# Attention row maxima: the third one of a step as two 256-key halves, one on each half of TensorE

## The chip, the cores and the metric

The kernel runs on one core of a Trainium2 chip. The metric is the device time of one execution in microseconds (us), the median over several runs. Engines are called as in the profile: PE is TensorE (PEld its weight loads), DVE VectorE, ACT ScalarE, POOL GpSimd, SP the engine that issues most DMAs.

## The reference

Two layers of two sublayers each run over one activation of 2048 tokens by 512 features: a Fourier mixing sublayer (phase A below) and a multi-query attention (phase B). All arithmetic is float32. The attention has 32 query heads of width 16 that share one key head and one value head:

```python
q = (x @ wq).reshape(B, S, H, Dh).transpose(0, 2, 1, 3)
k = x @ wk
v = x @ wv
scores = jnp.einsum("bhqd,bkd->bhqk", q, k) * (Dh ** -0.5)
p = softmax(scores)
o = jnp.einsum("bhqk,bkd->bhqd", p, v)
x = x + o.transpose(0, 2, 1, 3).reshape(B, S, H * Dh) @ wo      # x was layer-normalised before
```

The softmax needs the largest score of every query row and head before the exponentials: 2048 x 32 row maxima over 2048 keys each.

## The kernel before

**Tiling.** The 2048 queries are 16 tiles of 128 rows. The 32 heads are 16 pairs (`NPAIR`): the query tile of a pair holds one head of it (g = 0) on partitions 0 to 63 and the other (g = 1) on partitions 64 to 127. The key tile `kz` is there twice in the same way. So a score matmul contracts over 64 partitions and uses one half of PE's rows, and a matmul of the other head can run beside it on the other half.

**Two passes over the scores.** A first set of matmuls, with queries as weights and keys streaming, serves the maxima alone: `max_half` (lines 347 to 351) computes 128 queries x 512 keys of one head into a PSUM bank (L350), and DVE reduces the bank to one column of the partial maxima `mxp` (L351). Some maxima are computed in phase A (`max_pair`, L336 and L338). When a query tile has all its partials, `max_neg` reduces and negates them, and `max_rows` turns them with a PE transpose (L379) and writes them by DMA into spare rows of the query tile, so that the second pass has them subtracted by the matmul itself. The second pass, with keys as weights and queries streaming, computes transposed scores (`score`, L773), ACT takes the exponential of two of them in one instruction of 128 x 1024 (L776) into a probability tile, and `pv` (L787) multiplies it with the values: four matmuls of 32 columns in each of two parts, eight in the profile, which use all 128 rows of PE.

**Steps.** Phase B is a loop of 512 steps a layer, 32 steps for each query tile (`phase_b`, line 908). A step handles one block of 128 keys and 16 of the heads. PE's program order in it is: the `pv` of the step two before; then the step's group of scores and maxima; then whatever tasks are due. The group is written out in lines 924 to 929:

```python
g = units[o.done][2] if o.done < len(units) else 1
for j, m in ((1 - g, 1), (g, 2), (3 - g, 0), (2 + g, 1)):
    score(i, s_, j)
    for _ in range(m):
        if owed(n) >= 1:
            more_max()
```

Scores 0 and 1 form the first ACT instruction of the step, 2 and 3 the second; `j % 2` is the half of PE. `units` (line 738) lists the maxima still owed, heads alternating, and `owed` allows three of them a step. So a group is: score on half 1-g, maximum on g, score on g, maximum on 1-g, maximum on g, score on 1-g, score on g: four matmuls on half g and three on the other, and the halves change roles from step to step. In the last tile, once the maxima are used up, scores 2 and 3 go to single banks (L766, L768).

**PSUM.** The eight banks are two pairs for the scores (`pair`, tag x; so scores 2 and 3 of a step need the pair that ACT read for scores 2 and 3 of the step before), three single banks (`bank`, tag y) for maxima, transposes and the output projection, and one for `pv` (tag z). A bank is given to the next tile of its tag when the last reader is done; `o_proj` (line 842) holds one y bank while it takes four maxima through the other two.

**Tasks beside the steps.** `half_tasks` and `out_tasks` (lines 959 to 970) list, by step of a tile, the work on finished query tiles: storing and reloading the attention output by SP's DMAs, its scaling and its split into two parts on POOL (`o_scale` L827, `o_hi` L833 and L834), the projection on PE at step 12 (`o_proj`, L86 to L88), the residual (`o_add`, L852) and the output DMA (L853; on POOL's queue in the first layer, on SP's in the second), and in the first layer the next layer norm (`o_stats`, `o_rstd`, `o_ln`, `o_xnh`, `o_xnl`: L166 to L182, L898, L902). `max_neg` comes at step 27 and `max_rows` at step 29, for the first and last query tile in two halves of eight head pairs. DVE, ACT, POOL and SP each work through their own queue in program order.

## Time and profile before

| | |
|---|---|
| three timed runs | 3717.65, 3720.38, 3726.05 us; median 3720.38 us |
| the profiled execution | 3724.12 us, its span 3722.3 us |
| phase B of the two layers (first `pv` to last) | 692.0 to 1864.4 us and 2542.7 to 3711.4 us of the span |
| mean granted PE clock | 0.990 of full speed; 1.00 in phase B |

The profile gives busy time and instruction counts by engine, groups of instructions by line with the mean duration of one, what ended an engine's idle time, and a timeline. In the timeline a row is one run of like instructions: start, length until the last one's end, engine, line, output and inputs, and how many. A matmul's row starts when it may enter PE; its end is modelled. "x" and "y" in the names are the bank tags; `slot` and `xnl` are query or probability tiles.

### The profile page before, as it was taken

Reading aid. Unit: us, or ns where it says so; the run is one execution under the profiler, and the core shown is the slowest. Engines: PE = TensorE matmul, PEld = TensorE weight load, DVE = VectorE, ACT = ScalarE, POOL = GpSimd, SP = SyncE. Lnnn points to the kernel's source line nnn. Section 1 sums busy time; section 2 is a strip of 40 time slices with the busy share of each in tenths; the row PEclk is TensorE's granted clock in tenths of the full one; section 3 lists DMA queues with packets and bytes.
Section 4 is the critical chain, followed back from the end, with each engine's and each line's share of the span. In section 5 each row is a group of like instructions: output and inputs, shape, how many; then the busy total and the mean of one; then the engine's idle time right before and its main releaser. Section 6 shows DMA issues by size and latency. Waiting matters only on the chain. (4 is left out here: it accounts for less than half of the span.)

```text
span 3722.3 us, 64512 instructions
## 1 busy us (share of the span) xinstructions
PE 3631.1 (98%) x25474; PEld 1909.3 (51%) x25474; DVE 2798.4 (75%) x4767; ACT 2400.3 (64%) x3104; POOL 777.3 (21%) x984
## 2 busy tenths in 40 slices
PE   8999999999999999999999999999999999999999
PEld 6786768533433333334377766684343334333333
DVE  5167978788888888888311779778888888888882
ACT  4322222688888888888933231227888888888888
POOL 5534332111111111111154342421000000000000
PEclk9999999999999999999999999999999999999999
DMA  5444241311111100110143342313111111001100
GB/s 176 133 136 125 97 119 52 101 32 50 33 36 31 49 22 24 33 47 23 40 131 104 129 124 92 110 64 89 47 33 36 33 49 34 22 22 50 33 24 25
DMA packets 204736, 243.00 MB, mean 65 GB/s; under 512 B 36880, under 2 KB 160784, under 8 KB 197264
## 3 DMA queue, kind: packets, MB, share of 16 engines
q1 hardware_dynamic: 199504, 222.08, 20.1%
q0 software_dynamic: 4864, 16.78, 1.5%
q8 instruction: 199, 3.26, 0.4%
q14 instruction: 105, 0.86, 0.1%
q10 hardware_dynamic: 64, 0.02, 0.0%
HBM read 174.58 MB, written 63.17 MB: 64 GB/s over the span
## 5 line engine op out<-in xcount | busy, mean ns | idle before, releaser
L776 ACT ACTIVATE slot<-x 128x1024 f32<-128x1024 f32 x1990 | 1943.1, 1027 | 334.4 <-PE x L773 265.5
L351 DVE TENSOR_REDUCE mxp<-y 128x1 f32<-128x512 f32 x3040 | 1908.1, 684 | 281.5 <-PE y L350 233.3
L787 PE MATMUL z<-slot,v 128*32 128x512 f32 x8192 | 1096.3, 605 | 1.9 <-ACT row L790 1.9
L773 PE MATMUL x<-slot,kz 64*128 64x512 f32 x2956 | 900.9, 447 | 3.6 <-DMA slot<-mt 3.5
L773 PEld LDWEIGHTS x<-slot,kz 64*128 64x128 f32 x2956 | 375.3, 185 | 731.5 <-ACT slot L776 598.5
L350 PE MATMUL y<-kz,slot 64*128 64x512 f32 x2208 | 726.2, 435 | 4.8 <-ACT mt L381 0.7
L338 DVE TENSOR_REDUCE mxe<-y 128x1 f32<-128x512 f32 x832 | 516.4, 682 | 189.4 <-PE y L336 184.7
L660 PE MATMUL x<-ch,xnh 64*128 64x512 f32 (+1 forms) x2048 | 507.8, 390 | 16.3 <-DVE slot L74 8.9
L660 PE MATMUL x<-ch,xnl 64*128 64x512 f32 (+1 forms) x2048 | 475.2, 369 | 0.0
L660 PE MATMUL x<-cl,xnh 64*128 64x512 f32 (+1 forms) x2048 | 474.7, 369 | 0.0
L350 PEld LDWEIGHTS y<-kz,slot 64*128 64x128 f32 x2208 | 349.5, 185 | 94.5 <-DVE mxp L351 27.5
L827 POOL TENSOR_TENSOR row<-row,row 128x256 f32<-128x256 f32 x63 | 46.3, 735 | 1677.8 <-DMA row<-rd 1422.6
L336 PE MATMUL y<-kz,slot 64*128 64x512 f32 (+1 forms) x1088 | 354.3, 420 | 33.7 <-DVE mxe L338 20.7
L78 POOL TENSOR_TENSOR cl<-craw,ch 128x512 fp32r<-128x512 f32 x236 | 303.1, 1303 | 289.2 <-ACT ch L77 229.3
L787 PEld LDWEIGHTS z<-slot,v 128*32 128x32 f32 x8192 | 163.6, 108 | 277.3 <-issue 249.2
L660 PEld LDWEIGHTS x<-ch,xnh 64*128 64x128 f32 x2048 | 268.7, 189 | 69.2 <-issue 16.4
L660 PEld LDWEIGHTS x<-ch,xnl 64*128 64x128 f32 x2048 | 280.7, 189 | 33.3
L660 PEld LDWEIGHTS x<-cl,xnh 64*128 64x128 f32 x2048 | 281.7, 190 | 28.0
L77 ACT CAST ch<-craw 128x512 fp32r<-128x512 f32 x256 | 154.8, 620 | 161.8 <-PE x L660 89.5
L666 ACT COPY junk<-x 128x2 f32<-128x2 f32 x256 | 40.5, 158 | 332.3 <-PE x L660 253.6
L336 PEld LDWEIGHTS y<-kz,slot 64*128 64x128 f32 x1088 | 171.8, 188 | 129.4 <-DVE mxe L338 90.5
L338 DVE TENSOR_REDUCE mxp<-y 128x1 f32<-128x512 f32 (+1 forms) x256 | 144.4, 617 | 24.7 <-PE y L336 21.5
(148 smaller groups left out, 3141.7 us busy)
## 6 DMA issues: line engine op xcount, KB each, us to landing
craw<-ct_in SPq DMA_DIRECT2D x112, 512.0 KB
slot<-qd SPq DMA_DIRECT2D x44, 1024.0 KB
qd<-row SPq DMA_DIRECT2D x144, 128.0 KB
od<-row SPq DMA_DIRECT2D x252, 64.0 KB
row<-x_in SPq DMA_DIRECT2D x32, 256.0 KB
mid<-row POOLq DMA_DIRECT2D x32, 256.0 KB, 2.4
craw<-ct_in SPq DMA_DIRECT2D x32, 256.0 KB
row<-mid SPq DMA_DIRECT2D x32, 256.0 KB
```

Of the source, the lines that this page charges most:

```text
L77: nc.scalar.copy(hi, raw)
L78: (eng or nc.vector).tensor_sub(lo, raw, f(hi))
L336: nc.tensor.matmul(pm[g], o.qT[i][gs, pr, :], kz[gs, c0:c0 + n], start=True, stop=True)
L338: nc.vector.reduce_max(to[:, g:g + 1], pm[g], axis=AX.X)
L350: nc.tensor.matmul(pm, o.qT[i][gs, pr, :], kz[gs, kb * 512:kb * 512 + 512], start=True, stop=True)
L351: nc.vector.reduce_max(partial(i)[:, pr, g, kb:kb + 1], pm, axis=AX.X)
L660: nc.tensor.matmul(z[d][:, cols], w, hl[j][t == 1][rs_], start=m == 0 and ph == 0 and j == t == 0, stop=j == 1 and t == 2 and (ph == 0 or ...
L666: nc.scalar.copy(junk, zp[dd][:, :, cols.start])
L773: nc.tensor.matmul(st["e"][:, g, :], kz[64 * g:64 * g + KR, c * P:(c + 1) * P], o.qT[i][64 * g:64 * g + KR, cp:cp + 4, :], start=True, sto ...
L776: nc.scalar.activation(ptiles[i, s_][:, 2 * w:2 * w + 2, :], st.pop("e"), AF.Exp, scale=DH ** -0.5)
L787: nc.tensor.matmul(a[32 * j:32 * j + 32, :], v1[:, c, :], pt[:, j, :], start=c == 0, stop=c == NT - 1)
L827: nc.gpsimd.tensor_mul(bt["ot"][:, cs], bt["ot"][:, cs], bt["den"][:, cs])
```

## The change

The third maximum of a step is replaced. A step now takes one whole pair of maxima, 512 keys for both heads of a pair (`max_both`, or `max_half` for each head), and one couple: 256 keys for both heads, the two results side by side in one y bank, reduced by one DVE instruction to two columns of the partials (`max_couple`). The fourth 512-key block of each tile but the first is done in couples ("split"), the others whole; the partials get a fifth column for the second 256 keys. The two matmuls of a couple write one bank from the two halves of PE, and the second is held back until the first is complete: a `nop` on POOL's queue waits for the first matmul, and the second matmul waits for the `nop` (`behind_`).

The group's order becomes: score 0, score 1, whole maximum on half 0, couple on half 1, score 3, score 2, whole maximum on half 1, couple on half 0. In steps named by `alone`, where POOL has other work queued, there is no couple: the old order is used, with one maximum of an "odd" pair, whose other head follows in a later such step. `pick_pair`, `pick_couple` and `pick_odd` choose the work; `pick_pair` also takes two halves as a whole 512-key block if a tile's due step ("at") comes too near.

Beside that: `o_scale` and `o_hi` come in one step (28 and 10 in place of 27/29 and 9/10), `o_ln` and `o_xnh` in step 25 and `o_xnl` in 26; the output DMA is an `o_out` of its own at step 13 on SP's queue; query tile 14 has its maxima turned in two halves too; a new partial tile has its fifth column set by a POOL memset; two small tiles (`ktmp`, `ms`) use the memory of others. The end of phase A takes its twelve maxima as six pairs. The core of the diff:

```diff
+HALVED = (0, NT - 2, NT - 1)
...
+    def behind_(later, first):
+        tc.add_manual_dep(later.ins, first.ins.name,
+                          mybir.DependencyInfo(mybir.DependencyClass.Sync, mybir.DependencyReason.DATA), reason="row halves")
...
 
         def partial(i):
             if i not in o.mxp:
-                o.mxp[i] = sb.tile([P, NPAIR, 2, 4 if i else 5], F32, name=f"mxp{i % 4}")
+                o.mxp[i] = sb.tile([P, NPAIR, 2, 5], F32, name=f"mxp{i % 4}")
+                if i:
+                    nc.gpsimd.memset(o.mxp[i][:, :, :, 4:5], -3.0e38)
                 for e, (i_, kb, *_) in enumerate(KEPT):
                     if i == i_:
                         nc.gpsimd.tensor_copy(o.mxp[i][:, :, :, kb], st["mxe"][:, e])
...
             gs = slice(64 * g, 64 * g + KR)
             nc.tensor.matmul(pm, o.qT[i][gs, pr, :], kz[gs, kb * 512:kb * 512 + 512], start=True, stop=True)
             nc.vector.reduce_max(partial(i)[:, pr, g, kb:kb + 1], pm, axis=AX.X)
+
+        def max_couple(i, pr, kb, h, g):
+            if g:
+                st["couple"] = bank("y").rearrange("p (g c) -> p g c", g=2)
+            gs = slice(64 * g, 64 * g + KR)
+            c0 = 512 * kb + 256 * h
+            mm = nc.tensor.matmul(st["couple"][:, g, :], o.qT[i][gs, pr, :], kz[gs, c0:c0 + 256], start=True, stop=True)
+            if g:
+                st["relay"] = nc.gpsimd.nop()
+                behind_(st["relay"], mm)
+            else:
+                behind_(mm, st.pop("relay"))
+                nc.vector.reduce_max(partial(i)[:, pr, :, 4 if h else kb], st.pop("couple"), axis=AX.X)
 
         def qT_load(i, k=None):
             k_ = QSLOT[i] if k is None else k
...
-        def max_neg(i, p0=0, n=NPAIR, k=4):
+        def max_neg(i, p0=0, n=NPAIR, k=5):
...
-            ms = sb.tile([P, 2, 2, NPAIR], F32, name="ms").rearrange("p g r a -> p (g r a)")
-            ms = ms[:, :4 * n].rearrange("p (g r a) -> p g r a", g=2, r=2)
+            ms = half(0 if i or p0 else 2)[:, :4 * n].rearrange("p (g r a) -> p g r a", g=2, r=2)
...
         early = {e[:2] for e in EARLY}
-        units = [(0, pr, g, 3) for pr in range(HALF, NPAIR) for g in range(2)]
-        units += [(i, pr, g, kb) for i in range(1, NT) for pr in range(NPAIR) for kb in range(4) for g in range(2)
-                  if (i, kb) not in early]
-        o.done = o.extra = 0
-
-        def more_max():
-            if o.done < len(units) and units[o.done][0] in o.loaded | {0}:
-                max_half(*units[o.done])
-                o.done += 1
-
-        def owed(n):
-            return min(3 * (n + 1) + 12 + o.extra, len(units)) - o.done
+        groups = {}
+        for i in range(NT):
+            for hf in range(2) if i in HALVED else (None,):
+                prs = range(NPAIR) if hf is None else range(HALF * hf, HALF * hf + HALF)
+                if i or hf:
+                    kbs = [kb for kb in range(4) if (i, kb) not in early] if i else [3]
+                    at = NSTEP * i + NT - AHEAD if hf else NSTEP * (i - 1) + NSTEP - AHEAD
+                    groups[i, hf] = {"at": at, "whole": [(pr, kb) for pr in prs for kb in kbs if kb < 3 or not i],
+                                     "split": [(pr, 3, h) for pr in prs for h in range(2) if i]}
+
+        def in_reach(j, n):
+            return j in o.loaded | {0} and (j <= 1 or n >= NSTEP * max(0, j - 4 if j < 13 else j - 2) + 8)
+
+        def alone(n):
+            i, s_ = divmod(n, NSTEP)
+            if i == 0 and 12 <= s_ < 20 or s_ == 29 or i > 0 and s_ == 11:
+                return True
+            return not last and i > 0 and s_ in (17, 18, 26, 27)
+
+        def pick_pair(n, until=0):
+            due = 0
+            for (j, _), g in groups.items():
+                if not in_reach(j, n):
+                    return None
+                if g["at"] < until:
+                    continue
+                if g["whole"]:
+                    pr, kb = g["whole"].pop(0)
+                    return j, pr, kb
+                due += len(g["split"])
+                if due > g["at"] - n and len(g["split"]) > 1:
+                    pr = g["split"].pop()[0]
+                    g["split"].pop()
+                    return j, pr, 3
+            return None
+
+        def pick_couple(n):
+            for (j, _), g in groups.items():
+                if not in_reach(j, n):
+                    return None
+                if g["split"]:
+                    return j, *g["split"].pop(0)
+            return None
+
+        def pick_odd(n):
+            if "odd" in st:
+                return *st.pop("odd"), 1
+            pick = pick_pair(n, next((m for m in range(n + 1, n + NSTEP) if alone(m) or m > 448), n + 1))
+            if pick:
+                st["odd"] = pick
+                return *pick, 0
+            return None
+
+        def max_both(j, pr, kb):
+            for g in range(2):
+                max_half(j, pr, g, kb)
 
         def done_with(i, pr):
-            return all(u[:2] > (i, pr) for u in units[o.done:])
+            if "odd" in st and st["odd"][0] <= i and st["odd"][1] <= pr:
+                return False
+            return not any(q <= pr for (j, _), g in groups.items() if j <= i for q, *_ in g["whole"] + g["split"])
+
+        def all_done():
+            return not any(g["whole"] or g["split"] for g in groups.values()) and "odd" not in st
 
         ptiles = {}
 
...
-            if i == NT - 1 and jj == 1 and o.done == len(units):
+            if i == NT - 1 and jj == 1 and all_done():
...
                 o_mm(k)
                 if k % 2 and i < NT - 1:
-                    for _ in range(2):
-                        more_max()
-                        o.extra += 1
+                    pick = pick_pair(NSTEP * (i + 1) + 12)
+                    if pick:
+                        max_both(*pick)
             o_add(i)
 
         def o_add(i):
             nc.vector.tensor_add(bt["x"], bt["po"], bt["x"])
-            (nc.sync if last else nc.gpsimd).dma_start(dst[i], bt["x"])
+
+        def o_out(i):
+            nc.sync.dma_start(dst[i], bt["x"])
 
         def finish():
             i = NT - 1
...
                 if len(behind) == 2:
                     pv(*behind.pop(0))
                 behind.append((i, s_))
-                g = units[o.done][2] if o.done < len(units) else 1
-                for j, m in ((1 - g, 1), (g, 2), (3 - g, 0), (2 + g, 1)):
-                    score(i, s_, j)
-                    for _ in range(m):
-                        if owed(n) >= 1:
-                            more_max()
+                whole = pick_pair(n)
+                couple = None if alone(n) else pick_couple(n)
+                if not couple:
+                    odd = pick_odd(n)
+                    g = odd[3] if odd else 1
+                    score(i, s_, 1 - g)
+                    if whole:
+                        max_half(*whole[:2], g, whole[2])
+                    score(i, s_, g)
+                    if whole:
+                        max_half(*whole[:2], 1 - g, whole[2])
+                    if odd:
+                        max_half(*odd[:2], g, odd[2])
+                    score(i, s_, 3 - g)
+                    score(i, s_, 2 + g)
+                else:
+                    score(i, s_, 0)
+                    score(i, s_, 1)
+                    if whole:
+                        max_half(*whole[:2], 0, whole[2])
+                    max_couple(*couple, 1)
+                    score(i, s_, 3)
+                    score(i, s_, 2)
+                    if whole:
+                        max_half(*whole[:2], 1, whole[2])
+                    max_couple(*couple, 0)
                 if i == 0 and 2 <= s_ <= 8 and s_ % 2 == 0:
                     q_half_store(14, s_ // 2 - 1)
                 if n == 12:
...
-                for at, j, p0, np_ in ((NT - AHEAD, i, HALF, HALF), (NSTEP - AHEAD, i + 1, 0, HALF if i == NT - 2 else NPAIR)):
-                    if j in (0, NT - 1) or j == i + 1 < NT:
+                for at, j, p0, np_ in ((NT - AHEAD, i, HALF, HALF),
+                                       (NSTEP - AHEAD, i + 1, 0, HALF if i + 1 in HALVED else NPAIR)):
+                    if j in HALVED or j == i + 1 < NT:
...
-                            assert done_with(j, p0 + np_ - 1)
-                            max_neg(j, p0, np_)
+                            assert done_with(j, p0 + np_ - 1), (n, j, p0, groups)
+                            max_neg(j, p0, np_, 5 if j else 4)
...
         def half_tasks(i):
             return {
                 18: [lambda: o_store(i, 0)], 19: [lambda: o_sum(i, 0)], 22: [lambda: o_inv(i, 0)],
-                23: [lambda: o_load(i, 0)], 27: [lambda: o_scale(i, 0)], 29: [lambda: o_hi(i, 0)],
+                23: [lambda: o_load(i, 0)], 28: [lambda: o_scale(i, 0), lambda: o_hi(i, 0)],
             }
 
         def out_tasks(i):
             return {
                 1: [lambda: o_store(i, 1), lambda: o_sum(i, 1), lambda: x_load(i)], 5: [lambda: o_inv(i, 1)],
-                6: [lambda: o_load(i, 1)], 9: [lambda: o_scale(i, 1)], 10: [lambda: o_hi(i, 1)],
-                12: [lambda: o_proj(i)], 14: [lambda: o_stats(i)], 16: [lambda: o_rstd(i)],
-                25: [lambda: o_ln(i)], 26: [lambda: o_xnh(i)], 27: [lambda: o_xnl(i)],
+                6: [lambda: o_load(i, 1)], 10: [lambda: o_scale(i, 1), lambda: o_hi(i, 1)],
+                12: [lambda: o_proj(i)],
+                13: [lambda: o_out(i)], 14: [lambda: o_stats(i)], 16: [lambda: o_rstd(i)],
+                25: [lambda: o_ln(i), lambda: o_xnh(i)], 26: [lambda: o_xnl(i)],
             }
 
         woh = wol = osp = None
```

More of the change, by code (lines that the diff above doesn't have):

```diff
@@ L100, in fnet_mqa_kernel @@
     kmask = sb.tile([P, 1], F32, name="kmask")
-    t_ = sb.tile([P, 1], F32, name="ktmp")
+    t_ = junk[:, :1]
     nc.vector.tensor_reduce(kone[:64], ident[:64, M0:M0 + 2], op=ALU.add, axis=AX.X)
@@ L730, in phase_a @@
                     v_tr(12, 4, vt[0])
-            max_neg(0, 0, HALF, 5)
-            for k in range(12):
-                more_max()
-                if k == 2:
+            max_neg(0, 0, HALF)
+            for k in range(6):
+                max_both(*pick_pair(0))
+                if k == 1:
                     max_rows(0, 0, HALF, nc.scalar)
         early = {e[:2] for e in EARLY}
-        units = [(0, pr, g, 3) for pr in range(HALF, NPAIR) for g in range(2)]
-        units += [(i, pr, g, kb) for i in range(1, NT) for pr in range(NPAIR) for kb in range(4) for g in range(2)
-                  if (i, kb) not in early]
@@ L879, in finish @@
             o_add(i)
+            o_out(i)
         o.finish = finish
```

1 line of the change is left out of this document (removed).

## The prediction

> **What bounds the kernel now.** I read the page first: the shares of the engines and the costliest groups.
>
> ```profile
> PE 3631.1 (98%) x25474; PEld 1909.3 (51%) x25474; DVE 2798.4 (75%) x4767; ACT 2400.3 (64%) x3104; POOL 777.3 (21%) x984
> ...
> L776 ACT ACTIVATE slot<-x 128x1024 f32<-128x1024 f32 x1990 | 1943.1, 1027 | 334.4 <-PE x L773 265.5
> L351 DVE TENSOR_REDUCE mxp<-y 128x1 f32<-128x512 f32 x3040 | 1908.1, 684 | 281.5 <-PE y L350 233.3
> L787 PE MATMUL z<-slot,v 128*32 128x512 f32 x8192 | 1096.3, 605 | 1.9 <-ACT row L790 1.9
> ```
>
> PE looks like the bound, and eight L787 matmuls a step make 8192 / 8 = 1024 steps, and by the table above phase B is 2341 of the 3722 us. But overlapping matmuls make a busy share say little, so I went to the timeline of one step in the second layer (start, length, engine, line, count):
>
> ```profile
> 3003.89 0.39 PE L773 MATMUL x<-slot,kz 64*128 64x512 f32 x1
> ...
> 3003.93 0.18 PEld L350 LDWEIGHTS y<-kz,xnl 64*128 64x128 f32 x1
> 3004.12 1.89 DVE L351 TENSOR_REDUCE mxp<-y 128x1 f32<-128x512 f32 x3 [0.24 <-PE x L773]
> 3004.24 0.19 PEld L773 LDWEIGHTS x<-slot,kz 64*128 64x128 f32 x2
> 3004.24 0.51 PE L773 MATMUL x<-slot,kz 64*128 64x512 f32 x2
> 3004.38 1.94 ACT L776 ACTIVATE slot<-x 128x1024 f32<-128x1024 f32 x2 [0.19 <-PE y L350]
> ...
> 3004.68 1.06 PE L787 MATMUL z<-slot,v 128*32 128x512 f32 x8
> ...
> 3005.68 0.50 PE L773 MATMUL x<-slot,kz 64*128 64x512 f32 x1
> ...
> 3005.68 0.49 PE L350 MATMUL y<-kz,xnl 64*128 64x512 f32 x1
> ...
> 3006.02 0.39 PE L773 MATMUL x<-slot,kz 64*128 64x512 f32 x1
> 3006.02 0.63 PE L350 MATMUL y<-kz,xnl 64*128 64x512 f32 x2
> ...
> 3006.24 1.29 DVE L351 TENSOR_REDUCE mxp<-y 128x1 f32<-128x512 f32 x2 [0.24 <-PE x L773]
> 3006.37 0.19 PEld L773 LDWEIGHTS x<-slot,kz 64*128 64x128 f32 x2
> 3006.37 0.51 PE L773 MATMUL x<-slot,kz 64*128 64x512 f32 x2
> 3006.50 1.03 ACT L776 ACTIVATE slot<-x 128x1024 f32<-128x1024 f32 x1 [0.18 <-PE y L350]
> ```
>
> Call the start of a group, its first score, G: here 3005.68. The step is 3006.37 - 3004.24 = 2.13 us. Two things hold it there at once.
>
> *PE's fuller half.* The half with four matmuls starts them at G, +0.34, +0.58 (3006.02 + 0.63 - 0.39 = 3006.26) and +0.81 (3006.37 + 0.51 - 0.39 = 3006.49): 0.23 to 0.24 each, and the first 0.34, because its weight load of about 0.50 - 0.39 = 0.11 is not covered after the `pv`. The next `pv` would start 0.32 after that, and from `pv` to G it is 3005.68 - 3004.68 = 1.00: 0.81 + 0.32 + 1.00 = 2.13.
>
> *A loop through ACT.* Scores 2 and 3 need the pair of banks that ACT read for scores 2 and 3 of the step before. ACT's two instructions from 3004.38 end at 3004.38 + 1.94 = 3006.32, and the weight load of the third score starts at 3006.37: PE waited for that bank. Round the loop: G to ACT's start 0.82; ACT 1.94; to PE 0.05; third score to the next `pv` 0.44 (3004.24 to 3004.68); `pv` to G 1.00. That is 4.25 over two steps, 2.13 a step. Both limits give the same step, so shortening only one of them gains nothing.
>
> DVE needs 1.89 of the 2.13 and is not behind.
>
> **The change part by part.** *How many steps.* By the code's lists the 16 tiles leave 15 x 16 x 2 = 480 couples a layer; taken through step by step they make 386 steps with a whole pair and a couple in the first layer and 432 in the second (818), 10 steps a layer with a couple alone, 94 and 48 in the old order, and 21 a layer with no maxima.
>
> *PE's halves.* Each half now has two scores, one whole maximum and one of 256 keys: 3.5 slots for 4. Half a slot, 0.12, times 818 is 94 us, the most that the change can bring.
>
> *The ACT loop.* The tail of the layer, where two scores are already issued together at G, shows what pairing does:
>
> ```profile
> 1831.07 0.50 PE L773 MATMUL x<-slot,kz 64*128 64x512 f32 x2
> ...
> 1831.40 0.40 PE L766 MATMUL y<-slot,kz 64*128 64x512 f32 x2
> ...
> 1831.67 1.03 ACT L776 ACTIVATE slot<-x 128x1024 f32<-128x1024 f32 x1
> ...
> 1831.73 1.06 PE L787 MATMUL z<-slot,v 128*32 128x512 f32 x8
> ```
>
> ACT starts at G + 0.60, 0.22 sooner than now. But the new order puts a whole maximum behind score 3 on the same half. Score 3 waits for ACT, so its weight load is uncovered: 0.34 to the maximum (as from 3005.68 to 3006.02), and from there to `pv` 0.33 (1831.40 to 1831.73): 0.67 where it was 0.44. Round the new loop: 0.60 + 1.94 + 0.05 + 0.67 + 1.00 = 4.26, 2.13 a step. The 0.22 won at the front is given back behind ACT. Price: 818 x 0.00 = 0.
>
> *PE alone in the new order.* If ACT were early, score 3 could start once the couple's first half has left: 0.34, then the next load begins 0.04 later (3003.89 to 3003.93) and takes 0.11: G + 0.49. The maximum follows at 0.72, `pv` at 1.05, a step of 2.05. PE is then no longer the limit, by 0.08.
>
> *The relay.* The couple's first matmul starts at G + 0.33, has half of the columns and ends at about +0.62 (0.39 less half a slot, 0.11, is 0.28). Then POOL must see it, do the `nop`, and PE must see that. The nearest rows are an operation that POOL starts after ACT, and a PE start after POOL:
>
> ```profile
> 718.74 0.62 ACT L77 CAST slot<-row 128x512 fp32r<-128x512 f32 x1
> ```
> ```profile
> 719.44 1.29 POOL L78 TENSOR_TENSOR slot<-row,slot 128x512 fp32r<-128x512 f32 x1 [36.49 <-ACT slot L77]
> ```
> ```profile
> 44.00 1.29 POOL L480 TENSOR_TENSOR xnl<-row,xnh 128x512 fp32r<-128x512 f32 x1 [1.07 <-ACT xnh L479]
> ```
> ```profile
> 45.34 0.50 PE L88 MATMUL x<-ch,xnl 128*128 128x512 f32 x1
> ```
>
> ACT ends at 719.36 and POOL starts 0.08 later; POOL ends at 45.29 and PE starts 0.05 later. From PE to an engine I take 0.08 to 0.12 (ACT starts 0.10 after a score's end, 1831.07 + 0.50 to 1831.67). The trace has no `nop`; the shortest POOL operation is 0.19 (below), so it is between 0 and 0.19, and I take 0.04, near the low end, because it moves no data. The second matmul's load can then start at 0.62 + 0.10 + 0.04 + 0.05 = 0.81. Score 3 starts at 0.60 + 1.94 + 0.05 - 2.13 = 0.46, so by its path `pv` comes at 0.46 + 0.67 = 1.13. By the couple's path it comes at the load + 0.11 + 0.33, less 0.11 for the half slot: the load may be as late as 0.80. So the relay just about fits. Between a `nop` of 0 with the short wait (0.75) and one of 0.19 with the long (0.98) the price is 0 to 0.18 a step, 0 to 147 us; I take 0.005, 4 us, near the `nop` of 0.04. All PE work after the couple, the next `pv` first, is queued behind that wait, and DVE's third reduction waits for it.
>
> *POOL's other work.* A `nop` behind POOL's tasks would be late by their length.
>
> ```profile
> L182 POOL TENSOR_SCALAR row<-row,mv,rs 128x512 f32<-128x512 f32 x15 | 31.2, 2077 | 1.5
> L834 POOL TENSOR_TENSOR slot<-row,slot 128x256 fp32r<-128x256 f32 x31 | 23.0, 741 | 2.5
> L827 POOL TENSOR_TENSOR row<-row,row 128x256 f32<-128x256 f32 x31 | 22.8, 736 | 626.5 <-DMA row<-rd 492.3 <-PE x L773 122.0 <-PE y L350 12.1
> L902 POOL TENSOR_TENSOR xnl<-row,xnh 128x512 fp32r<-128x512 f32 x15 | 19.3, 1286 | 1.3
> L833 POOL CAST slot<-row 128x256 fp32r<-128x256 f32 x31 | 12.4, 399 | 1.9
> L853 POOL DMA_DIRECT2D res<-row x15 | 9.3, 619 | 189.0 <-DVE row L852 189.0
> L898 POOL CAST xnh<-row 128x512 fp32r<-128x512 f32 x15 | 9.2, 612 | 1.0
> L173 POOL TENSOR_TENSOR lnw<-rs 128x1 f32<-128x1 f32 x45 | 8.6, 192 | 117.3 <-DVE rs L166 115.0
> ```
>
> `o_scale` and `o_hi` take 0.74 + 0.40 + 0.74 = 1.88 and have the one step of 2.13 after them free of couples; the layer norm's 2.08 + 0.61 + 1.29 = 3.98 have two; `o_rstd`'s twelve operations of 0.19 have two. Moving `o_scale` a step later costs nothing: POOL sits waiting for its loads now (492 of the 626 us), and they get a step more. The output DMA leaves POOL, 0.62 fifteen times, for SP's queue, where it waits for the DVE addition; behind it SP has `o_store` five steps later. If this cover failed, a late relay would hold PE for what is left of the task, at most the 1.88 twice a tile, 2 x 31 x 1.88 = 117 us. I cost it at nothing.
>
> *Change of order.* In an old-order step ACT starts at G + 0.82; if a new-order step follows, its score 3 waits until 0.69 and the step is 0.69 + 0.67 + 1.00 = 2.36, 0.23 too long; the step after may give back up to 0.08 (floor 2.05). Such changes, apart from those after `max_rows`, number three a tile in the first layer and one in the second: about 57 x 0.17 = +10 us. After other long steps ACT is early, and the next step saves up to 0.08, half of it kept: some 90 times, -3 us.
>
> *Tail.* L766 ran 58 times a layer, so 29 steps had no maxima; now 21 have none and ten a couple alone. The rows below, from the first layer's phase B, give the tail's count and the transposes:
>
> ```profile
> L766 PE MATMUL y<-slot,kz 64*128 64x512 f32 x58 | 17.4, 441 | 0.5 <-DVE mxp L351 0.4
> L379 PE MATMUL y<-ident,ms 128*64 128x128 f32 (+1 forms) x17 | 5.0, 296 | 0.0
> ```
>
> A step without maxima saves at most 0.23 (one slot), a step with a couple alone about 0.06: 2 x (8 x 0.23 - 10 x 0.06) = +3 us. The added `max_neg` and `max_rows` of tile 14 cost a transpose of 0.30 and a DVE wait of the same order, twice: +1. The rest (memset, shared memory, pairs at the end of phase A) is beside other work or the same work: 0.
>
> **Sum.** 0 + 4 + 10 - 3 + 3 + 1 = +15 us on the profiled 3724; the median of the runs is 3.7 lower: 3735 us.
>
> **The rivals.** *PE decides* (faster). If the wait for ACT is softer than the rows say, the step falls to PE's 2.05: 818 x -0.08 = -65, about 3660; half of that is 3690. For it: PE at 98%, one half of it with four matmuls. Against it: the third score's load starts 0.05 after ACT's end.
>
> *The relay is late* (slower still). If the couple's first matmul is only reported when the whole maximum issued just before it ends, at 0.33 + 0.39 = 0.72 and not at 0.62, the relay is 0.10 later, the step 2.22 to 2.26: +75 to +105, about 3810. It decides once PE waits for the relay longer than 0.18 after the couple's first matmul ends. In this trace matmuls that overlap have one length, so nothing speaks for or against. The Trainium skill ("TensorE: Matmul & The Clock Gate", Part 3, The mechanism) has this as a rule: matmuls end in program order, whatever the tile. By that rule the sum is this rival's; no row here shows it.
>
> *The couple's bank.* If a couple took the bank of the couple before, it would wait for DVE's third reduction: the whole maximum ends at 0.72, DVE starts at 0.80 and needs 1.89, to 2.74 with the hand-over, 2.74 - T in the next step of length T; from there 0.22 to score 3, 0.23 and 0.33 to `pv`, 1.00 to G: T = 2.26, 818 x 0.13 = +106, about 3830. The code speaks against it: `o_proj` holds one bank over four maxima, so banks go by release, and the couple gets the one freed second.
>
> *The change does not do what it says.* If few steps took couples it would be the old kernel, 3720; the lists say otherwise.
>
> **How the numbers follow.** About 0.2% (7.4 us) is what a measurement of this kernel can tell. The forecast, the loop holds and the relay about fits, has 0.55, with 3715 to 3755 of its own; PE decides, in part or whole, 0.22; the relay late 0.16; the bank 0.04; no change in fact 0.03. The forecast's share is split 0.03 faster, 0.17 same, 0.35 slower; the faster rival's 0.20 and 0.02. Faster 0.23, same 0.22, slower 0.55. The range 3685 to 3800 leaves out the deeper half of the faster rival and the later part of the slower ones, about 0.18.
>
> **What would show it.** Right: in plain steps ACT starts 0.60 after the group's first score (0.82 before), the third score's load still 0.05 after ACT's end and now near G + 0.47, and `pv` starts stay 2.13 apart; steps behind an old-order one near 2.36. The relay is hidden if the couple's second load starts by G + 0.80. Wrong: `pv` starts 2.05 to 2.10 apart (PE decided), or PE idle before the couple's second matmul, put down to POOL, with steps of 2.2 or more.

## The result and the profile after

The changed kernel takes 3756.09 us (median of four runs, 3755.72 to 3757.24), the kernel before 3722.21 us beside it (four runs, 3717.65 to 3726.05): a ratio of 1.0092 (1.0075 to 1.011), 34 us slower. The profiled execution took 3755.72 us, its span is 3753.9 us.

The page of the changed kernel, engines and the groups that answer to those shown of before (busy us, mean ns | idle us before them and what ended it):

```profile
PE 3663.0 (98%) x26314; PEld 1976.3 (53%) x26314; DVE 2808.9 (75%) x4773; ACT 2397.4 (64%) x3092; POOL 770.3 (21%) x998
...
L844 ACT ACTIVATE slot<-x 128x1024 f32<-128x1024 f32 x2004 | 1950.0, 1026 | 377.2 <-PE x L841 340.3
L358 DVE TENSOR_REDUCE mxp<-y 128x1 f32<-128x512 f32 x2202 | 1416.4, 686 | 309.4 <-PE y L357 292.0
...
L371 DVE TENSOR_REDUCE mxp<-y 128x2 f32<-128x512 f32 x838 | 572.6, 683 | 27.6 <-PE y L365 27.6
...
L365 PEld LDWEIGHTS y<-kz,slot 64*128 64x128 f32 x1228 | 227.8, 185 | 85.7 <-POOLq L367 71.4
```

ACT's exponential (L844, before L776) and DVE's reductions (L358, and L371 for the couples) last what they did: 1026 ns, and 686 and 683. The busy shares tell nothing. The new thing is the last row: the weight loads of couples whose queries lie in `slot` wait 71.4 us for the `nop` of line 367. A few hundredths of a microsecond at each of 838 couples is what one looks for here.

The timeline of the changed kernel at the place that was shown of before (start, length, engine, line, count; in brackets the idle time before and what ended it):

```profile
3003.69 1.02 ACT L844 ACTIVATE slot<-x 128x1024 f32<-128x1024 f32 x1
...
3004.41 0.50 PE L841 MATMUL x<-slot,kz 64*128 64x512 f32 x2
...
3004.74 0.39 PE L357 MATMUL y<-kz,xnl 64*128 64x512 f32 x1
3004.75 0.28 PE L365 MATMUL y<-kz,slot 64*128 64x256 f32 x1
3004.76 0.19 PEld L841 LDWEIGHTS x<-slot,kz 64*128 64x128 f32 x2
...
3005.01 1.94 ACT L844 ACTIVATE slot<-x 128x1024 f32<-128x1024 f32 x2 [0.30 <-PE x L841]
...
3005.27 0.18 PEld L365 LDWEIGHTS y<-kz,slot 64*128 64x128 f32 x1 [0.20 <-POOLq L367]
...
3005.58 1.07 PE L855 MATMUL z<-slot,v 128*32 128x512 f32 x8
...
3006.58 0.50 PE L841 MATMUL x<-slot,kz 64*128 64x512 f32 x2
...
3007.45 0.18 PEld L365 LDWEIGHTS y<-kz,slot 64*128 64x128 f32 x1 [0.16 <-POOLq L367]
...
3007.76 0.64 PE L855 MATMUL z<-slot,v 128*32 128x512 f32 x4
```

G is 3004.41. The couple's first matmul ends at 3005.03 (G + 0.62) and the whole maximum, issued one instruction before it, at 3005.13 (G + 0.72). The second matmul's load comes at G + 0.86: 0.24 after the end of its own first half, 0.14 after that of the whole maximum. `pv` follows at G + 1.17 and the next group 1.00 later. The step is 2.17 to 2.18 (`pv` 3005.58 to 3007.76), where it was 2.13. ACT is in time (its instruction ends at 3004.71, the third score's load follows 0.05 later): score 3 still waits for it, but by the prediction's 0.67 from that load `pv` could start at 3005.43, 0.15 before it does.

Where the 34 us are: from each layer's first `pv` to its last, phase B takes 1192.7 and 1189.5 us where it took 1172.3 and 1168.6, +41.2 together. 642 of its steps (293 and 349) were between 2.09 and 2.15 and are now between 2.15 and 2.205; they give +34.9, 0.054 each. All others together give +6.3. The rest of the span came out 9.7 us shorter in this execution. Phase A of the second layer was 678.4 us in the profile of before and 670.5 to 676.3 in those of all other kernels of this case, among them 674.2 in one that has the phase A of before (e9, below); so I take most of the 9.7 for spread between executions, not for a gain.

### The profile page after: what moved, and what is told of

Its sections match the earlier page's. It is cut to its first block, busy times and chain, and to the rows that moved or that the text cites. A ratio compares the mean times of both kernels' runs of the same rounds, so it can differ in the third digit from the quotient of the medians.

```text
span 3753.9 us, 67192 instructions
## 1 busy us (share of the span) xinstructions
PE 3663.0 (98%) x26314; PEld 1976.3 (53%) x26314; DVE 2808.9 (75%) x4773; ACT 2397.4 (64%) x3092; POOL 770.3 (21%) x998
## 5 line engine op out<-in xcount | busy, mean ns | idle before, releaser
L844 ACT ACTIVATE slot<-x 128x1024 f32<-128x1024 f32 x2004 | 1950.0, 1026 | 377.2 <-PE x L841 340.3
L358 DVE TENSOR_REDUCE mxp<-y 128x1 f32<-128x512 f32 x2202 | 1416.4, 686 | 309.4 <-PE y L357 292.0
L841 PE MATMUL x<-slot,kz 64*128 64x512 f32 x2984 | 762.0, 461 | 2.2 <-DMA slot<-mt 2.0
L841 PEld LDWEIGHTS x<-slot,kz 64*128 64x128 f32 x2984 | 304.1, 184 | 730.0 <-ACT slot L844 614.5
L357 PE MATMUL y<-kz,slot 64*128 64x512 f32 x1594 | 602.2, 413 | 3.8 <-DVE mxp L358 1.5
L371 DVE TENSOR_REDUCE mxp<-y 128x2 f32<-128x512 f32 x838 | 572.6, 683 | 27.6 <-PE y L365 27.6
L679 PE MATMUL x<-ch,xnh 64*128 64x512 f32 (+1 forms) x2048 | 500.0, 386 | 18.5 <-DVE slot L79 10.4
L679 PE MATMUL x<-cl,xnh 64*128 64x512 f32 (+1 forms) x2048 | 466.9, 364 | 0.0
L365 PE MATMUL y<-kz,slot 64*128 64x256 f32 x1228 | 401.3, 327 | 0.0
L357 PEld LDWEIGHTS y<-kz,slot 64*128 64x128 f32 x1594 | 281.4, 186 | 51.8 <-DVE mxp L371 18.1
L895 POOL TENSOR_TENSOR row<-row,row 128x256 f32<-128x256 f32 x63 | 46.1, 732 | 1251.6 <-PE x L841 1015.3
L365 PEld LDWEIGHTS y<-kz,slot 64*128 64x128 f32 x1228 | 227.8, 185 | 85.7 <-POOLq L367 71.4
```

The costliest lines, as they stand in the source:

```text
L357: nc.tensor.matmul(pm, o.qT[i][gs, pr, :], kz[gs, kb * 512:kb * 512 + 512], start=True, stop=True)
L358: nc.vector.reduce_max(partial(i)[:, pr, g, kb:kb + 1], pm, axis=AX.X)
L365: mm = nc.tensor.matmul(st["couple"][:, g, :], o.qT[i][gs, pr, :], kz[gs, c0:c0 + 256], start=True, stop=True)
L371: nc.vector.reduce_max(partial(i)[:, pr, :, 4 if h else kb], st.pop("couple"), axis=AX.X)
L679: nc.tensor.matmul(z[d][:, cols], w, hl[j][t == 1][rs_], start=m == 0 and ph == 0 and j == t == 0, stop=j == 1 and t == 2 and (ph == 0 or ...
L841: nc.tensor.matmul(st["e"][:, g, :], kz[64 * g:64 * g + KR, c * P:(c + 1) * P], o.qT[i][64 * g:64 * g + KR, cp:cp + 4, :], start=True, sto ...
```

## The experiments

Two theories of the late load were on the table. **A**: the couple's first matmul is reported only after the whole maximum issued before it, although it ends sooner. **B**: a hand-over through POOL simply takes 0.2. Besides, whether ACT's loop or PE's halves hold the step once the relay is hidden. All kernels ran beside the kernel before; where nothing else is said, they do all its work.

### e1: the couple ahead of the whole maximum

```diff
+                    max_couple(*couple, 1)
                     if whole:
                         max_half(*whole[:2], 0, whole[2])
-                    max_couple(*couple, 1)
```

> The couple's first matmul is issued ahead of the whole maximum that stood before it (both start on their own half of PE at the same time either way). Theory A, ends in program order: its end is now reported right after score 1, POOL's nop comes 0.11 us earlier, the couple's second load starts by G + 0.78 and the wait is hidden; plain steps go from 2.18 to 2.13 us (the ACT loop), about 730 x -0.05, so 3717 us. Theory B, POOL's path itself takes 0.18 us from the matmul's end: second load still at G + 0.86, 2.18 us a step, 3756. If PE and not the ACT loop decides once the relay is gone: 2.05 us a step, below 3680.

Measured: 3732.05 us (3729.01 to 3736.2), ratio to before 1.0035 (1.0023 to 1.0048). Two swapped instructions give back 24 of the 34 us. In the trace's single events the `nop` starts 0.038 us after the couple's first matmul ends (765 of 838, 0.074 before the whole maximum's end), where in the changed kernel it starts 0.185 after its own and 0.073 after the whole maximum's end (781). In the changed kernel's 57 couples without a whole maximum ahead it is 0.038 too. Nor does POOL just wait for a count that takes in both matmuls: in none of the 781 does the semaphore (the counter) that PE raises for finished matmuls step between the two ends, and in e1 it does so in all 765. So the end is reported in program order, and theory B falls: the way through POOL is short (0.038, the `nop`'s 0.017, 0.051 to PE's load). The ends in the rows are modelled, so the trace does not tell whether the shorter matmul ends late or is only reported late; for the wait it is the same. The excess over the whole maximum's end, 0.073 against 0.038, goes with there being two ends to report at once: in the 781 the counter's two steps lie 0.034 apart. The Trainium skill states both ("TensorE: Matmul & The Clock Gate", Part 3, The mechanism, that matmuls end in program order; The cost: per-tile semaphore tail, that reports serialize, 26 ns each); the trace agrees with the first as far as the reports go, and shows 34 ns for the second.

The steps of e1, two of them in its timeline:

```profile
2993.76 3.97 ACT L844 ACTIVATE slot<-x 128x1024 f32<-128x1024 f32 x4 [0.27 <-PE x L841]
...
2993.88 0.18 PEld L365 LDWEIGHTS y<-kz,slot 64*128 64x128 f32 x1
...
2994.20 1.06 PE L855 MATMUL z<-slot,v 128*32 128x512 f32 x8
...
2995.76 0.19 PEld L841 LDWEIGHTS x<-slot,kz 64*128 64x128 f32 x2 [0.26 <-ACT slot L844]
...
2996.42 1.07 PE L855 MATMUL z<-slot,v 128*32 128x512 f32 x8
...
2998.02 1.02 ACT L844 ACTIVATE slot<-x 128x1024 f32<-128x1024 f32 x1 [0.28 <-PE x L841]
```

The couple's second load no longer waits for POOL. The step from 2994.20 is 2.22 and the ones beside it are 2.03 (medians by place in the tile: 2.03 and 2.22, in turn). Their sum is 4.25, the loop through ACT over two steps: ACT works 3.97 without a gap and waits 0.28. The loop bounds a pair of steps, not each one: PE takes one of them in 2.03 and waits for ACT in the other (0.26 before 2995.76). So e1 is at the same 2.125 as before, and theory A's 3717 was missed by 15 because long steps grew: step 29 of the second layer, the one with the transposes, from 2.57 to 3.28 (+9 us; e3 and e5 below), and steps 18, 19 and 28 of the first layer as in the changed kernel (+6).

### e2 and e3: the paired order also in steps without a couple

The old-order steps take score 0, score 1, whole maximum, odd maximum, scores 2 and 3, whole maximum; e2 does this to the changed kernel, e3 to e1.

> The steps without a couple get the new order too: scores 0 and 1 together, a whole maximum and the odd one, the two other scores, the second whole maximum. Theory A (ACT starts late in an old-order step, and the next step pays for it): the 86 steps of 2.34 us behind such steps fall to 2.18, -14 us, 3742. Rival: these steps are long because POOL's own work delays the relay; then they stay and the time is 3756.

> Both edits. Theory A: plain steps 2.13 and no long steps behind the old order; -39 and -18 us, about 3700 to 3712, a little under the kernel before, because the steps behind a PE stall got shorter by the change. Theory B for the relay: as the run with the second edit alone, 3742. If PE decides: below 3670.

Measured: e2 3754.33 us (3752.45 to 3758.86), ratio 1.0096 (1.0082 to 1.011); e3 3737.17 us (3729.55 to 3738.15), 1.0044 (1.0031 to 1.0056). Both miss. In e2 the steps behind old-order ones fall as expected (steps 28 and 19 of a tile in the first layer: from 2.35 and 2.25 to 2.18), but step 29, where `max_rows` transposes, rises from 2.54 to 2.74 there: phase B gains 4 us in all. In e3 step 29 is 3.23 to 3.28 in both layers. The views of line 392 (`max_neg`'s subtraction on DVE; shortest, median and longest ns), of e3 and then of the changed kernel:

```profile
L392 DVE TENSOR_TENSOR row<-nm,row x38: 174/620/740, 679.7 to 3681.8; 128x32 fp32r<-128x32 f32 x26, 128x16 fp32r<-128x16 f32 x12
```
```profile
L392 DVE TENSOR_TENSOR row<-nm,row x38: 174/192/194, 677.9 to 3698.7; 128x32 fp32r<-128x32 f32 x26, 128x16 fp32r<-128x16 f32 x12
```

What it collides with, in the timeline of e1's second layer:

```profile
3346.04 0.73 POOL L895 TENSOR_TENSOR row<-row,row 128x256 f32<-128x256 f32 x1 [41.32 <-PE y L357]
3346.21 0.61 DVE L392 TENSOR_TENSOR row<-nm,row 128x32 fp32r<-128x32 f32 x1
```

POOL's `o_scale` runs to 3346.77, and DVE's subtraction ends at 3346.82. Who starts first decides: in e1 the 14 subtractions that begin after `o_scale` take 0.60 to 0.72, the 12 that begin before it 0.19; in the changed kernel all 13 that meet it begin first.

### e4: pairs alone, no couples

```diff
-                    groups[i, hf] = {"at": at, "whole": [(pr, kb) for pr in prs for kb in kbs if kb < 3 or not i],
-                                     "split": [(pr, 3, h) for pr in prs for h in range(2) if i]}
+                    groups[i, hf] = {"at": at, "whole": [(pr, kb) for pr in prs for kb in kbs], "split": []}
...
         def alone(n):
...
+            return True
```

with e2's order in every step, so the third maximum is whole again.

> No couples at all: every step takes a whole pair and one odd maximum of 512 keys, in the paired order of scores. One half of PE has four slots again, so both limits of the kernel before stand: 2.13 us a step, 3722 +- 8 us. If pairing the scores by itself were a gain (ACT starts 0.22 us earlier in each step) it would be faster by up to 40 us; if it were the cause of the loss, 3750 or more.

Measured: 3723.19 us (3717.89 to 3726.45), ratio 1.0009 (1.0 to 1.0018); plain steps 2.12 to 2.13. The pairing, and everything else that came with the change, costs nothing in the plain steps and at most 7 us in all (the interval's end); the rest of the 34 us belongs to the couples.

### e5: `o_scale` and `o_hi` out of DVE's way

On e3: both a step later in all but the last tiles, and with them the step without a couple (one more such step keeps the odd heads even).

```diff
-            if i == 0 and 12 <= s_ < 20 or s_ == 29 or i > 0 and s_ == 11:
+            if i == 0 and 12 <= s_ < 20 or s_ == (30 if i < NT - 2 else 29) or n == 455 or i > 0 and s_ == 11:
...
-                23: [lambda: o_load(i, 0)], 28: [lambda: o_scale(i, 0), lambda: o_hi(i, 0)],
+                23: [lambda: o_load(i, 0)], 29 if i < NT - 2 else 28: [lambda: o_scale(i, 0), lambda: o_hi(i, 0)],
```

> The version of e3 (couple ahead of the whole maximum, paired order in the steps without a couple), and besides o_scale and o_hi of the first half one step later, at step 29, so that POOL's scaling no longer runs beside DVE's subtraction in max_neg (the steps without a couple move with it, from 29 to 30). Theory: e3's step 29 of 3.2 to 3.3 us comes from that overlap (DVE's operation of 0.61 us where it has 0.19 alone), so the step returns to some 2.6 to 2.8, about 0.5 us in 30 tiles: e3's 3737 becomes 3717 to 3725, the time of the kernel before. Rival: the long step is the transpose's own wait in the new order, and the time stays at 3732 to 3740.

Measured: 3723.3 us (3718.71 to 3726.78), ratio 1.001 (1.0001 to 1.0018). The view of line 392 in e5:

```profile
L392 DVE TENSOR_TENSOR row<-nm,row x38: 174/192/742, 678.0 to 3664.7; 128x32 fp32r<-128x32 f32 x26, 128x16 fp32r<-128x16 f32 x12
```

The median is 192 ns again, step 29 falls to 2.89, and 14 us come back. With relay and collision gone, the couples end where the old kernel was: the loop through ACT, 2.03 and 2.22 in turn.

### e6 and e7: ACT's second instruction in two

In e6 (on e5) and e7 (on the kernel before) the second pair's exponential is two instructions of 512 columns.

```diff
-                st["e"] = pair()
...
-                nc.scalar.activation(ptiles[i, s_][:, 2 * w:2 * w + 2, :], st.pop("e"), AF.Exp, scale=DH ** -0.5)
+            if "xp" not in st:
+                st["xp"] = [pair(), pair()]
+            e = st["xp"][w]
...
+            if w == 0:
+                nc.scalar.activation(ptiles[i, s_][:, 0:2, :], e, AF.Exp, scale=DH ** -0.5)
+            else:
+                for b in (1 - g, g):
+                    nc.scalar.activation(ptiles[i, s_][:, 2 + b, :], e[:, b, :], AF.Exp, scale=DH ** -0.5)
```

> The version of e5, and besides ACT's second instruction of a step is two of one bank each, the two pairs of banks kept by a layer, so that score 3 of the next step waits for the first of the two alone. Theory: with the relay hidden the step is bound by the loop through ACT (4.25 us over two steps) and PE's halves need 2.03 to 2.05 alone; releasing a bank some 0.4 us earlier takes the loop off the path and the steps go to 2.05 to 2.10: 25 to 60 us less than e5, 3665 to 3700. Rival: PE is bound by something else at 2.12 (the profile only puts it down to ACT), or ACT's added fixed cost fills it: within 8 us of e5, or slower.

> The kernel before with ACT's second instruction in two, as in e6, and nothing else. Theory (two limits of the same length: PE's half with four matmuls, and the loop through ACT): the loop is loosened, PE's half stays at 2.13, so no gain: 3715 to 3730. Rival: the loop through ACT alone bound the kernel before, and this gains as much as in e6, 3690 or less.

Measured: e6 3747.48 us (3745.48 to 3750.82), ratio 1.0075 (1.0062 to 1.0088); e7 3741.95 us (3741.63 to 3749.73), 1.0064 (1.0049 to 1.0078). Neither expectation held for e7, and e6 went the rival's way. The timelines of e6 and of e7 tell why:

```profile
3006.05 1.02 ACT L848 ACTIVATE slot<-x 128x1024 f32<-128x1024 f32 x1 [0.27 <-PE x L842]
...
3006.97 1.08 ACT L851 ACTIVATE slot<-x 128x512 f32<-128x512 f32 x2
...
3008.11 0.18 PEld L842 LDWEIGHTS x<-slot,kz 64*128 64x128 f32 x2 [0.32 <-ACT slot L851]
```
```profile
3004.82 1.02 ACT L780 ACTIVATE slot<-x 128x1024 f32<-128x1024 f32 x1 [0.18 <-PE x L774]
...
3005.74 1.08 ACT L783 ACTIVATE slot<-x 128x512 f32<-128x512 f32 x2
...
3006.88 0.19 PEld L774 LDWEIGHTS x<-slot,kz 64*128 64x128 f32 x2 [0.19 <-ACT slot L783]
```

In e6 both score loads come at 3008.11, 0.06 after the second instruction's end (3006.97 + 1.08 = 3008.05), although score 3 needs the bank that the first one read. Of e6's 980 pairs of such instructions all but one have only the second raise the semaphore that PE waits for: the two banks are one tile, and it is given back whole. In e7 it is the same: ACT's work ends at 3006.82, 2.00 after its start (it was 1.94), and both loads come 0.06 later. (In e7 the halves change roles from step to step, so the next step's first score takes the bank that is read second: e7 could not have loosened the loop in any case.) So the edit did not release a bank sooner; it only made ACT longer by 0.06. That alone lengthens every second step by 0.06 (2.12 and 2.18 in e7, 2.03 and 2.28 in e6) and costs 23 to 24 us in both kernels: the loop through ACT is on the path of either.

### e8: four nops in place of one

```diff
-                st["relay"] = nc.gpsimd.nop()
-                behind_(st["relay"], mm)
+                behind_(nc.gpsimd.nop(), mm)
+                nc.gpsimd.nop()
+                nc.gpsimd.nop()
+                st["relay"] = nc.gpsimd.nop()
+                behind_(st["relay"], mm)
```

> The changed kernel with four nops on POOL's queue in place of one between the couple's two matmuls. Theory: the relay decides the step, so every 0.01 us that it takes more is 8 us of time; a nop of 0.017 and what lies between two of them make 0.05 to 0.15 for the three more: 3795 to 3880. Rival: the relay ends beside a wait that is as long anyway, and the time stays near 3756 or rises by less than 15.

Measured: 3755.56 us (3752.02 to 3756.74), ratio 1.0093 (1.0077 to 1.0108). This says nothing on either theory: the trace has 838 nops, as before, all of line 370. The three that nobody waits for are not in the program, and the run is a repeat of the changed kernel.

### e9, e10, e11: a shorter ACT

ACT's instructions of 1024 columns are cut to 896, in the kernel before (e9), the changed one (e10) and e5 (e11). The exponentials of 64 columns of each bank are left out, with a constant in their place.

```diff
-                nc.scalar.activation(ptiles[i, s_][:, 2 * w:2 * w + 2, :], st.pop("e"), AF.Exp, scale=DH ** -0.5)
+                nc.scalar.activation(ptiles[i, s_][:, 2 * w:2 * w + 2, :448], st.pop("e")[:, :, :448], AF.Exp, scale=DH ** -0.5)
```

> The kernel before with ACT's instructions over two score banks cut from 1024 to 896 columns (the exponentials of the other 64 columns of each bank are left out, a constant stands in their place; three probability tiles kept through a layer for that); PE and DVE keep all their work. By the rows of 128x1024 (1.03) and 128x512 (0.60) ACT's two instructions take 1.73 in place of 1.94. Theory (two limits of one length): PE's half with four matmuls holds the step at 2.12 to 2.13: 3710 to 3725. Rival: the loop through ACT alone held it: 2.03 or so, 3620 to 3640.

> The changed kernel with ACT's instructions cut to 896 columns in the same way, the relay as it is. Theory (the relay, reported late, holds PE on a path of its own: pv at G + 1.17 whatever ACT does): steps stay at 2.16 to 2.18, 3740 to 3757. Rival: the plain step of 2.18 is still a loop through ACT, lengthened: it falls by about 0.1 a step, 3655 to 3690.

> The version of e5 (couple ahead of the whole maximum, relay hidden) with ACT's instructions cut to 896 columns in the same way. Theory: with relay and ACT out of the way PE's halves of 3.5 slots set the step: 2.03 to 2.06, 55 to 85 us under e5's 3723: 3640 to 3668. Rival: something else (the relay, DVE) holds it at 2.12: 3715 to 3725.

Measured: e9 3699.66 us (3695.55 to 3701.49), ratio 0.9947 (0.9934 to 0.9961); e10 3739.6 us (3736.26 to 3742.41), 1.0053 (1.0038 to 1.0069); e11 3666.91 us (3666.35 to 3672.84), 0.9864 (0.9851 to 0.9878). Two instructions take ACT 1.73 in place of 1.94 in all three.

The timelines of e9, e10 and e11:

```profile
3005.09 1.73 ACT L779 ACTIVATE slot<-x 128x896 f32<-128x896 f32 x2 [0.38 <-PE y L350]
3005.39 0.16 PEld L790 LDWEIGHTS z<-slot,v 128*32 128x32 f32 x8 [0.36 <-issue]
...
3007.50 1.07 PE L790 MATMUL z<-slot,v 128*32 128x512 f32 x8
```
```profile
3005.04 0.18 PEld L365 LDWEIGHTS y<-kz,slot 64*128 64x128 f32 x1 [0.16 <-POOLq L367]
...
3005.35 1.06 PE L858 MATMUL z<-slot,v 128*32 128x512 f32 x8
...
3007.22 0.18 PEld L365 LDWEIGHTS y<-kz,slot 64*128 64x128 f32 x1 [0.16 <-POOLq L367]
...
3007.53 1.06 PE L858 MATMUL z<-slot,v 128*32 128x512 f32 x8
```
```profile
2984.84 1.06 PE L858 MATMUL z<-slot,v 128*32 128x512 f32 x8
...
2986.87 1.06 PE L858 MATMUL z<-slot,v 128*32 128x512 f32 x8
2987.81 0.68 DVE L371 TENSOR_REDUCE mxp<-y 128x2 f32<-128x512 f32 x1
...
2988.54 0.18 PEld L357 LDWEIGHTS y<-kz,xnl 64*128 64x128 f32 x1
...
2988.63 1.29 DVE L358 TENSOR_REDUCE mxp<-y 128x1 f32<-128x512 f32 x2
...
2988.97 1.06 PE L858 MATMUL z<-slot,v 128*32 128x512 f32 x8
...
2989.84 0.68 DVE L371 TENSOR_REDUCE mxp<-y 128x2 f32<-128x512 f32 x1
```

The first stays at 2.11 (median 2.12): PE's half with four matmuls holds it. The 20 us that e9 gains, more than expected, come mainly from the steps after long ones (steps 1 and 2 of a tile: 2.17 and 2.28 to 2.12) and from the tail (1.90 to 1.79). The second stays at 2.18, with PE waiting for the `nop` as before: the relay is a path of its own and has nothing to do with ACT. e10's 16 us under the changed kernel come mainly from the tail and from steps beside long ones, such as step 28 of the first layer (2.35 to 2.18). The third falls to 2.03 and 2.10 (medians by place 2.04 and 2.09), 56 us under e5.

The longer of e11's two steps is not PE's own floor. Its second whole maximum waits for the y bank that DVE's couple reduction of the step before gives back: the reduction ends at 2988.49 and the maximum's load comes at 2988.54, and it comes 0.04 to 0.06 after that reduction in all but one of e11's 311 couple steps of 2.08 to 2.12 us. This is a third loop over two steps, through DVE: the reductions start 0.76 after G (2987.87) and take 1.89, the load comes 0.05 later, `pv` 0.43 after it, and the next G 1.00 after that: 4.13, which is 2.04 + 2.09. In the steps of 2.03 `pv` comes 0.31 after the couple's second load, as in the changed kernel, so there the relay may be the limit again; no run shows PE's halves alone. With the relay hidden and ACT shortened the couples buy 33 us (e9 against e11), 0.055 a step of the 0.12 that half a slot is.

### e12: two single banks for the second scores

On e5, with all work done: scores 2 and 3 have banks of their own (tag u, taken from the second pair) and an ACT instruction of 512 columns each, so that score 3 waits for one bank alone. In phase A the second pair of banks becomes two single ones as well, which splits some of its small copies in two.

```diff
-        return ps.tile([P, 2, 512], F32, name="x", bufs=2)
+        return ps.tile([P, 2, 512], F32, name="x", bufs=1)
...
+            if w:
+                e = bank("u")
+                nc.tensor.matmul(e, kz[64 * g:64 * g + KR, c * P:(c + 1) * P],
+                                 o.qT[i][64 * g:64 * g + KR, cp:cp + 4, :], start=True, stop=True)
+                nc.scalar.activation(ptiles[i, s_][:, j, :], e, AF.Exp, scale=DH ** -0.5)
+                return
```

> The version of e5 with scores 2 and 3 in single banks of their own, each with its own ACT instruction of 512 columns, so that score 3 waits for one bank's exponential and not for two (in e6 the tile's release still came with the second). All the work is done. Theory: ACT frees score 3's bank about 0.5 sooner and score 2's 0.06 later, and behind score 2 stands half a slot less to pv: the loop is 0.60 + 2.00 + 0.05 + 0.56 + 1.00 = 4.21, 2.105 a step, some 15 to 25 us under e5: 3698 to 3710, below the kernel before. Rival: ACT's longer pair or the added small copies of phase A eat it: 3718 or more.

Measured: 3709.42 us (3705.91 to 3715.33, 11 runs), ratio 0.9974 (0.9965 to 0.9983): 11 us faster than the kernel before, 47 us faster than the changed one, and within the expected 3698 to 3710. Its timeline:

```profile
3005.76 1.06 PE L877 MATMUL z<-slot,v 128*32 128x512 f32 x8
3006.24 1.08 ACT L858 ACTIVATE slot<-u 128x512 f32<-128x512 f32 x2
...
3007.10 0.45 PEld L856 LDWEIGHTS u<-slot,kz 64*128 64x128 f32 x2
...
3007.91 1.06 PE L877 MATMUL z<-slot,v 128*32 128x512 f32 x8
```

The two score loads (L856) are 0.45 from the first one's start to the second one's end: the first goes at 3007.10, while ACT still reads the other bank, and the second (a load lasts 0.18) at about 3007.37, 0.05 after ACT's end at 3007.32. Only score 2 waits now, and 0.54 later `pv` starts, where it took 0.66 behind score 3 in e1 (2995.76 to 2996.42). The steps are 2.03 and 2.16 in turn, 2.095 in the mean.

## Why the prediction was right, and where it was not

The direction was right, and the range held the time. The size was not: +15 was forecast, +34 measured, just outside the forecast's own 3715 to 3755. Nor was the main mechanism: that ACT's loop holds the step and the relay about fits had 0.55, and what held the step was the relay, the rival of 0.16. That both pointed to a slower kernel is in part luck, since 10 of the forecast's 15 us were changes of order.

*PE's halves.* Four slots at 2.13 in the old order: e9 shows 2.12. Right. The new order's floor was put at 2.05; the shortest steps of e1 and e11, 2.03, do not contradict it, but no run shows PE alone. The prediction had DVE "not behind" at 1.89 of 2.13 and left out the loop through the bank of its third reduction, 4.13 over two steps, which e11 runs into.

*The ACT loop.* ACT starts 0.60 after G (3004.41 to 3005.01), the third score's load 0.05 after ACT's end, and the loop is 4.25 over two steps in e1, where 4.26 was worked out. Price 0: right, and e5 agrees, where this loop is the limit; e6 and e7 show that lengthening ACT lengthens the steps. Two limits of one length was right too: taking ACT's away leaves PE's (e9), taking PE's away leaves ACT's (e5), taking both gains (e11).

*The relay.* This step failed: "so the relay just about fits", a load at G + 0.81 against a bound of 0.80, priced at +4 us. The load came at G + 0.86. Of the four terms the couple's own end (0.62) and the hand-over to PE (0.05) were right and the `nop` shorter than taken (0.017 for 0.04). The wait from PE to POOL, taken as 0.10 after the couple's end, was 0.185, because the report came after the whole maximum's. Excess 0.06, 0.054 a step over 642 steps: +34.9 us. The rest of the 818 steps with a whole pair and a couple are in the sum of all other steps, +6.3. PE idle before the couple's second matmul and put down to POOL was the sign of being wrong that the prediction named, though the steps are 2.18 and not 2.2 or more.

*The rival "the relay is late"* had this mechanism, its place and the rule behind it, and its chance of 0.16 was too low. Its price was too high: it put the load at 0.91 and charged all 818 steps with the excess, +75 to +105. A short `nop` and a hand-over of 0.073 where 0.10 was assumed make half of that. "PE decides" fell: ACT's loop was as hard as the rows said, until e11 took it away. The couple does not wait for the bank of the couple before; the second whole maximum does (in the changed kernel its load mostly comes 0.05 after the couple reduction, at about G + 0.53), and 0.43 from there to `pv` makes 0.96, well before 1.17: no cost until e11.

*POOL's other work.* Right at nothing: all but two of the 838 `nop`s start within 0.20 us of the end of the couple's first matmul, those two within 0.29. The groups of the changed kernel by line (both layers; `o_scale`, `o_hi`, and the tail's scores in single banks):

```profile
L902 POOL TENSOR_TENSOR slot<-row,slot 128x256 fp32r<-128x256 f32 x63 | 46.7, 741 | 5.0
L895 POOL TENSOR_TENSOR row<-row,row 128x256 f32<-128x256 f32 x63 | 46.1, 732 | 1251.6 <-PE x L841 1015.3 <-PE y L357 164.8 <-DMA row<-rd 39.8
L834 PE MATMUL y<-slot,kz 64*128 64x512 f32 x88 | 26.5, 437 | 0.7 <-DVE mxp L358 0.7
```

`o_scale` waits for its loads only 39.8 of 1251.6 us now, and steps 10 and 11 of a tile, where the second one and its free step lie, are 2.18 like the plain ones.

*Changes of order.* Predicted +10 less 3 for the steps after long ones. An old-order step before a couple step gives 2.35 at step 28 of the first layer, where 2.36 was worked out, but at step 19 it is 2.25, and step 16 falls from 2.50 to 2.36. Steps 16, 18, 19 and 28 of the first layer together: +4.8. In the second layer the long step with the transposes grew instead (2.57 to 2.76, +2.6). The tail (+2.2 in the last 34 steps of the two layers) was near its +3. All steps other than the 642 together, +6.3, are below the +11 forecast for order, tail and transposes.

Not tried: the changed order of matmuls with no relay at all, since the two halves then write one bank at once. Open: why step 29, 2.57 in the kernel before, is longer in every version with the paired order in the steps without a couple, whatever the plain steps are (2.74 in e2, 2.80 in e4, 2.89 in e5, 2.95 in e12); in e12 it costs 11 us.

## What to carry to other kernels

When one matmul's end releases a wait, look at what was issued just before it, not only at its own length: here a matmul of 256 columns behind one of 512 was reported 0.15 us late, and putting it first cost the plain step nothing. When two limits have one length, a change to one buys nothing and can only show its side costs; price a loop over as many steps as it spans, since the steps may alternate (2.03 and 2.22) around it. Price every loop, those through an engine that is not behind too: here the one through ACT took 4.25 us and the one through DVE's bank, next in line, 4.13. A tile of two banks was given back whole here: splitting the reader helps only if the tile is split with it.

## What the runs showed that was not expected

A DVE subtraction of two SBUF operands took 0.61 us in place of 0.19 when POOL had begun a two-operand instruction of 0.73 before it, and nothing more when DVE began first; moving POOL's work by one step was worth 14 us. The Trainium skill says that a VectorE instruction with two SBUF inputs contends with a GpSimd instruction that reads SBUF, and that the order of issue decides which one waits ("SBUF — State Buffer", Who interferes with whom); the trace agrees for the VectorE side, 0.61 us behind POOL and 0.19 ahead of it. And the way from PE through POOL's queue back to PE, with no data, is 0.038 + 0.017 + 0.051 = 0.106 us.
